# Attention on one core: zero-padded tails for scores and masks, a threshold on GpSimd, and the last tiles' logits moved into the loop

## The chip, the cores and the metric

One core of a Trainium2 chip runs the whole program. The metric is the time of one execution on the device in microseconds (us); lower is better. PE is the matrix engine, PEld its loading of stationary blocks, DVE the vector engine, ACT the scalar engine, POOL is GpSimd and SP issues most transfers. Each engine works through its own instructions in the order in which the program puts them.

## What is computed

Three stages follow one another: attention that keeps the 32 largest scores of a row, a mixture of experts whose tokens are handed out greedily by their logits, and a dense layer with a rational function. Only the first stage and the logits of the second are touched by the change.

```python
B, H, S, D = 4, 8, 576, 64            # attention
scores = q @ k.T / sqrt(D)
kth = np.partition(scores, -32, axis=-1)[..., -32:-31]
mask = scores >= kth
scores = np.where(mask, scores, -1e9)
attn = softmax(scores)                # exp(scores - max) / (sum + 1e-9)
x = (attn @ v).transpose(0, 2, 1, 3).reshape(B * S, H * D)   # 2304 x 512
logits = x @ w_gate                   # 2304 x 8, then greedy assignment
...
```

## The kernel before

**Units.** Two batches and two heads make a pass (`si`, eight of them), nine tiles of 128 queries a pass. A unit `u` is one tile with both heads; there are 72. The first head of a pair has its 64 dimensions in partitions 0 to 63, the second in 64 to 127, so both heads' scores can use the two halves of PE's rows at once. `TAIL` is 64, `MAIN` 512, `S` 576, `HS` 288.

**The loop.** `step(u)` (L1025) writes the instructions of one unit of every stage, so that the engines work on different units at a time. In the order of the program: ACT evacuates the scores of `u` (`st_evacuate`, L688); PE makes the scores of `u + 1` (`st_scores`, L673); PE turns one of five pieces of the next pass's q and k (`prepare`), which ACT copies a step later (`place`, L650); PE turns an older unit's scores and adds the mask to them (`st_transpose`, L834); DVE finds candidates (`st_candidates`, L729), and between its maxima `fill` slips in what stands in the list `later`; ACT and POOL make the window (`st_window`, L763); PE multiplies by v (`st_av`, L860); ACT and POOL make the mask (`st_weights`, L819).

**The tail of k.** The 576 keys are 512 and a tail of 64. `kT` holds 512 keys and then the tail for both heads. For the first head the scores are two matmuls of 288 columns. The second head's output wants the tail first, so it takes three, of 64, 224 and 288 (`COLS`, L228, and `TURNS`, L671): five in all.

**The mask.** Turning a unit takes nine blocks of 128 columns. The middle block (c = 4) holds the first head's tail and the second head's first 64 keys. Each block gets one transpose and one mask product with the diagonal `dg`; the middle block gets two products of half width (L844).

**The threshold.** Every third unit closes a group. From the window DVE computes the threshold `tau` and, with two operations more, the lower threshold `pn`, which ACT needs for the mask (L800 to L808). From unit 66 on each unit is a group of its own (`SG`).

**Logits.** When a tile's last pair of heads is done, the tile stands in `fresh` and then in `ready`. In units 7, 8 and 0 of a pass the loop takes one tile and computes its logits: four transposes (L912), ACT's copy and the sum of squares `xs` (L917, L919), four products (L925), DVE's copy into `lg` (L926). This happens for the first nine tiles. The last nine are done in `finish_attention` (L1094), where a small planner (`Flow`) orders the remaining work of the loop, the logits (`add_logits`, L1167) and filler work by assumed costs: three-step conversions of weights (L383 to L385) and sums of squares of weights (L306). The squares of these nine tiles come after the branch (L1473). The branch (L1303) asks whether any threshold was suspicious and reads that value on every engine; behind it the routing starts.

## Time and profile before

| | us |
|---|---|
| median of 3 runs (1241.02 to 1245.92) | 1241.24 |
| the profiled execution | 1241.38 |
| its span in the trace | 1239.6 |
| attention's loop ends (last scores done) | 416.9 |
| last instruction before the branch ends | 475.2 |
| first instruction behind the branch | 479.4 |

All times of rows count from the span's start. A row of the timeline gives start, duration, engine, line, operation, the tile that it writes and those that it reads, and how many were merged; in brackets stands how long the engine was idle before it and what it waited for. PE's durations overlap: the distance of two starts tells more than one duration. An fp32 matmul leaves two records.

### The profile page before, as it was taken

The page shows a single profiled execution, that of the slowest core. Times are in us where ns is not written, and L with a number is a line of the kernel's source. Part 1 is how long each engine was busy: PE and PEld are TensorE (multiplying, and loading weights), DVE is VectorE, ACT ScalarE, POOL GpSimd, SP SyncE. Part 2 cuts the span into 40 slices and gives each one's busy share as a digit, 9 for nine tenths or more (in the row PEclk, how much of TensorE's full clock was granted, in tenths as well). Part 3 has the DMA queues.
Part 4 walks back from the last instruction along what each step waited for, and adds up shares of the span by engine and source line. Part 5 has one row for each costly group of instructions (what it writes and reads, how often), then busy time and mean ns, then how long its engine had stood idle before and what let it go on. Part 6 is the DMA issues. An engine that isn't in the chain of part 4 may idle for free.

```text
span 1239.6 us, 27194 instructions
## 1 busy us (share of the span) xinstructions
PE 1130.0 (91%) x9879; PEld 915.3 (74%) x9879; DVE 1061.9 (86%) x4148; ACT 1019.4 (82%) x1802; POOL 375.0 (30%) x458
## 2 busy tenths in 40 slices
PE   5899999999999985884837999999999999999996
PEld 3688888888888863653625877888888888888784
DVE  6999999989898955885988979898989889897795
ACT  4899999989998985677999978888888788876684
POOL 4788777768677700001010001000101000001010
PEclk9899999999999996555868999999999999999998
DMA  5204112021100304611323222222122222100000
GB/s 124 51 10 152 41 28 50 11 50 34 27 2 2 137 2 178 234 52 55 122 88 106 99 88 88 88 82 75 32 76 88 88 74 62 41 1 21 1 20 20
DMA packets 81108, 80.63 MB, mean 65 GB/s; under 512 B 59968, under 2 KB 59968, under 8 KB 80960
## 3 DMA queue, kind: packets, MB, share of 16 engines
q1 hardware_dynamic: 77888, 69.27, 17.7%
q0 software_dynamic: 3072, 9.48, 2.6%
q8 instruction: 82, 1.34, 0.4%
q14 instruction: 66, 0.54, 0.1%
HBM read 69.25 MB, written 9.47 MB: 64 GB/s over the span
## 4 chain that ended last, share of the span: by engine, by line
PE 26%; issue 15%; ACT 7%; DVE 4%; POOL 1%; DMA 1%; POOLq 0%; DVEq 0%
PE pa L1922 3%; PE pa L1923 3%; PE pa L1924 3%; PE ph L1922 3%; PE ph L1924 3%; PE ph L1923 3%; PE po L1923 3%; PE po L1924 3%; PE po L1922 3%; ACT junk L306 2%; POOL out_dram L2308 1%; ACT w1s L1395 1%; PE pa L2297 0%; ACT wout L383 0%; DVE w2s L1400 0%
## 5 line engine op out<-in xcount | busy, mean ns | idle before, releaser
L774 POOL TENSOR_TENSOR win<-sv,sg 128x576 f32<-128x576 f32 x142 | 179.3, 1284 | 103.4 <-ACT sg L769 91.4
L738 DVE MAX8 cd<-sv 128x8 f32<-128x82 f32 (+1 forms) x1008 | 183.2, 230 | 11.2 <-ACT sv L691 8.7
L1922 PE MATMUL ph<-x,win 128*128 128x288 f16 x512 | 148.8, 291 | 10.5 <-DVE uv L2191 10.5
L873 PE MATMUL po<-vm,pT 128*128 128x65 f32 (+1 forms) x1280 | 150.5, 265 | 2.1 <-DVE x L893 1.5
L1923 PE MATMUL po<-g,wout 128*128 128x288 f16 x512 | 146.7, 287 | 2.4 <-DVE g L1913 2.4
L1924 PE MATMUL ph<-x,win 128*128 128x288 f16 x512 | 148.8, 291 | 0.0
L1923 PE MATMUL ph<-x,win 128*128 128x288 f16 x512 | 148.7, 290 | 0.0
L1922 PE MATMUL po<-g,wout 128*128 128x288 f16 x512 | 146.7, 287 | 0.9 <-ACT g L1912 0.8
L1924 PE MATMUL po<-g,wout 128*128 128x288 f16 x512 | 146.7, 286 | 0.0
L873 PEld LDWEIGHTS po<-vm,pT 128*128 128x128 f32 (+1 forms) x1280 | 138.6, 181 | 4.9 <-issue 2.1
L841 PE MATMUL pt<-ident,sv 128*128 128x128 f32 x648 | 132.0, 287 | 0.0
L845 PE MATMUL pt<-dg,mk 128*128 128x128 bf16 (+1 forms) x720 | 123.9, 225 | 0.0
L2308 POOL DMA_INDIRECT out_dram<-ob,tok x24 | 24.9, 1037 | 319.5 <-ACT ob L2304 267.5
L830 ACT ACTIVATE sg<-sv,pn 128x576 bf16<-128x576 f32 x136 | 97.8, 770 | 28.1 <-DVE pn L807 28.1
L1899 POOL DMA_INDIRECT xe<-xrows,rows_i x24 | 25.3, 1056 | 295.1 <-PE pa L1934 272.1
L769 ACT ACTIVATE sg<-sv,cut_all 128x576 bf16<-128x576 f32 x142 | 108.7, 774 | 6.2 <-DVE cut_all L744 6.1
L2182 ACT ACTIVATE z<-ph,inv 128x288 f32<-128x288 f32 x128 | 63.9, 499 | 58.7 <-PE ph L1924 57.9
L841 PEld LDWEIGHTS pt<-ident,sv 128*128 128x128 f32 x648 | 91.7, 141 | 20.8 <-issue 5.0
L775 DVE MAX8 w<-win 128x8 f32<-128x576 f32 x142 | 105.4, 743 | 0.0
L831 POOL TENSOR_SCALAR mk<-sg 128x576 bf16<-128x576 bf16 x136 | 89.5, 675 | 6.2 <-ACT sg L830 5.6
L855 ACT ACTIVATE pT<-pt 128x1152 f32<-128x1152 f32 x72 | 81.3, 1129 | 4.3 <-PE pt L845 4.0
L691 ACT ACTIVATE sv<-s 128x1152 f32<-128x1152 f32 x72 | 80.5, 1118 | 3.9 <-PE s L681 3.1
(362 smaller groups left out, 3333.2 us busy)
## 6 DMA issues: line engine op xcount, KB each, us to landing
region<-in_moe_w_dram SPq DMA_DIRECT2D x16, 2048.0 KB, 7.7
xrows<-x SPq DMA_DIRECT2D x1, 4644.0 KB
region<-in_q_dram SPq DMA_DIRECT2D x32, 128.0 KB, 2.6
region<-in_k_dram SPq DMA_DIRECT2D x32, 128.0 KB, 2.9
vm<-in_v_dram SPq DMA_DIRECT2D x32, 128.0 KB, 3.2
wout<-in_moe_w_in_dram SPq DMA_DIRECT2D x8, 511.8 KB, 8.0
region<-in_moe_w_out_dram SPq DMA_DIRECT2D x8, 511.8 KB, 3.5
win<-in_moe_w_in_dram SPq DMA_DIRECT2D x6, 511.8 KB, 7.8
```

The lines of the kernel that those rows point to most:

```text
L738: nc.vector.max(cd[:, g, :], sv[:, o : o + n])
L769: nc.scalar.activation(sg, sv_t[u, hh], AF.Sign, bias=cut_all[:, 2 * u + hh, 7:8], scale=-OVER, accum_out=t["sum"][:, c : c + 1],)
L774: nc.gpsimd.tensor_tensor(win, sv_t[u, hh], sg, op=OP.mult)
L775: later.append(lambda c=c, win=win: nc.vector.max(t["w8"][:, c, :], win))
L830: nc.scalar.activation(sg, sv, AF.Sign, bias=t["pn"][:, c : c + 1])
L831: nc.gpsimd.tensor_scalar(mk[:, hh, :], sg, -0.5, 0.5 + EPS, op0=OP.mult, op1=OP.add)
L841: nc.tensor.transpose(pt[:, c // 4, c % 4, :], pr[:, o : o + P], ident)
L845: nc.tensor.matmul(pt[p0 : p0 + n, c // 4, c % 4, :], mk[:, o + p0 : o + p0 + n], bat[b]["dg"][:, 2 * i + hh, :], start=False, stop=True, ...
L873: nc.tensor.matmul(po[p0 : p0 + n, i, hh, :], sb[:, hh * (R + 1) + c, p0 : p0 + n], vm[:, bb, hh, c, :], start=(c == 0), stop=False,)
L1922: nc.tensor.matmul(acc, ah, bh, start=first, stop=False)
L1923: nc.tensor.matmul(acc, ah, bl, start=False, stop=False)
L1924: nc.tensor.matmul(acc, al, bh, start=False, stop=last)
```

## The change

1. `kT` gets 640 columns: the tail stands behind the 512 keys for the first head and ahead of them for the second. Both heads then read two pieces of 288 columns, four matmuls for a unit. k's tail is copied in two instructions of 64 partitions. Both buffers of `kT` lie in `region`.
2. The mask of both heads lies in one of two fixed tiles with 64 columns of zeros between them. At the middle block both products are of full width: the first reads the first head's tail and the zeros, the second the zeros and the second head's first 64 keys.
3. `pn` is made by one POOL instruction from `tau`; two DVE operations a group go.
4. In the last pass every unit may take a tile's logits, and the last nine tiles count as ready once three of four pairs of heads are done. The loop then does three of four blocks of 128 columns. `finish_attention` adds the fourth block of these, and the whole of those not reached. The products there have 8 columns of output, without the turn back; the squares are done there too, those of the fourth block into `xs2`, added later.

```diff
     COLS = [
-        [(0, 0, 0, HS), (1, 0, HS, HS)],
-        [(0, 0, MAIN, TAIL), (0, TAIL, 0, HS - TAIL), (1, 0, HS - TAIL, HS)],
+        [(0, TAIL, HS), (1, TAIL + HS, HS)],
+        [(0, 0, HS), (1, HS, HS)],
     ]
...
-            kT_buf = [carve(8 * S + 2304, 2 * S), lp.tile([P, 2 * S], F32, name="kT", bufs=1)]
+            KW = S + TAIL
+            kT_buf = [carve(4 * S + 2 * KW * i, 2 * KW) for i in range(2)]
...
+            mk_buf = [wk.tile([P, 2 * S + TAIL], BF16, name=f"mk{i}", bufs=1) for i in range(2)]
+            for m in mk_buf:
+                nc.gpsimd.memset(m[:, S : S + TAIL], 0.0)
+
+            def mask_of(u, hh):
+                return mk_buf[u % 2][:, hh * (S + TAIL) : hh * (S + TAIL) + S]
...
-                    copy(kT[:, :, MAIN:S], ps[:, 1, :].rearrange("p (b c) -> p b c", b=2))
+                    tail = ps[:, 1, :].rearrange("p (b c) -> p b c", b=2)
+                    copy(kT[0:D, :, S:KW], tail[0:D])
+                    copy(kT[D:P, :, 0:TAIL], tail[D:P])
...
-            TURNS = [(1, 0), (0, 0), (1, 1), (0, 1), (1, 2)]
+            TURNS = [(1, 0), (0, 0), (1, 1), (0, 1)]
...
-                    rank, equal, lambda: pick("eqt", 1.0), lambda: pick("eqp", BEFORE),
-                    lambda: total("eqt", tau), lambda: total("eqp", t["pn"][:, g]),
+                def below():
+                    nc.gpsimd.tensor_scalar(t["pn"][:, g], tau, BEFORE, None, op0=OP.mult)
+
+                return [
+                    rank, equal, pick, total, below,
...
-                    for p0, n, hh in [(0, P, c // (R + 1))] if c != R else [(0, TAIL, 0), (TAIL, TAIL, 1)]:
+                    for hh, o in [(c // (R + 1), c * P + (TAIL if c > R else 0))] if c != R else [(0, MAIN), (1, S)]:
                         nc.tensor.matmul(
-                            pt[p0 : p0 + n, c // 4, c % 4, :], mk[:, o + p0 : o + p0 + n],
-                            bat[b]["dg"][:, 2 * i + hh, :], start=False, stop=True, skip_group_check=True,
+                            dst, mk_buf[u % 2][:, o : o + P], bat[b]["dg"][:, 2 * i + hh, :],
+                            start=False, stop=True, skip_group_check=True,
                         )
...
-                if hp == H // 2 - 1:
+                if hp == H // 2 - (1 if bp < B // 2 - 1 else 2):
                     fresh.extend(range(t0, t0 + n))
+                elif hp == H // 2 - 1:
+                    final.extend(range(t0, t0 + n))
...
+            def chunks_of(t):
+                return whole if t < NT - NJ else whole[: KC - 1]
...
-                pending = ready.pop(0) if ready and getting is None and j in (7, 8, 0) else None
+                pending = ready.pop(0) if ready and getting is None and (j in (7, 8, 0) or si == NSI - 1) else None
...
                 def add_logits(t, deps):
...
+                    cs = whole[KC - 1 :] if t in counted else whole
...
+                    def product():
+                        for i, c in enumerate(cs):
+                            nc.tensor.matmul(
+                                st["ps"][:, 1, 0:E], st["xt"][:, i, :], wg[:, c, :], start=(i == 0), stop=(c == last_c)
+                            )
+
+                    def leave():
+                        if n == 1:
+                            nc.vector.tensor_tensor(lg[:, t, :], st["ps"][:, 1, 0:E], lg[:, t, :], op=OP.add)
                         else:
...
-        norms = [
-            flow.add("A", 0.52, lambda t=t: square(x[:, t, 0:DM], xs[:, t : t + 1]), (), XSR) for t in late_tiles
-        ]
...
-            everywhere_steps(xs, OP.max, x_max) + [("V", 0.07, f) for f in power_steps(s_x, i_x, x_max, 388)],
-            norms, -85.0,
+            [("V", 0.1, lambda: nc.vector.tensor_tensor(xs, xs, xs2, op=OP.add))]
+            + everywhere_steps(xs, OP.max, x_max) + [("V", 0.07, f) for f in power_steps(s_x, i_x, x_max, 388)],
+            [], -85.0,
```

POOL, in the middle of the loop, around the end of a group (`win` is the window, `top_all` and `dg` the diagonal, `mk` the mask). Before:

```order
L774 TENSOR_TENSOR win<-sv,sg 128x576 x2
L757 TENSOR_SCALAR top_all<-top 128x6
L758 TENSOR_TENSOR dg<-identb,top_all 128x768
L831 TENSOR_SCALAR mk<-sg_691 128x576
L831 TENSOR_SCALAR mk<-sg_694 128x576
L774 TENSOR_TENSOR win<-sv,sg 128x576 x2
```

With the change:

```order
L787 TENSOR_TENSOR win<-sv,sg 128x576 x2
L770 TENSOR_SCALAR top_all<-top 128x6
L771 TENSOR_TENSOR dg<-identb,top_all 128x768
L844 TENSOR_SCALAR mk_172<-sg_683 128x576
L844 TENSOR_SCALAR mk_172<-sg_686 128x576
L821 TENSOR_SCALAR pn<-tau_all 128x6
L787 TENSOR_TENSOR win<-sv,sg 128x576 x2
```

`pn` stands behind the old group's masks and ahead of the next unit's two windows.

ACT, behind the loop, from the spill of `pT` for unit 67 to that for unit 68 and on to the next (L383 to L385 and L306 are filler). Before:

```order
L855 ACTIVATE pT<-pt 128x1152
L383 ACTIVATE win<-win 128x512 x2
L384 ACTIVATE win<-win 128x512 x2
L385 ACTIVATE win<-win,bias_111 128x512 x2
L383 ACTIVATE win<-win 128x512
L855 ACTIVATE pT<-pt 128x1152
L384 ACTIVATE win<-win 128x512
L306 ACTIVATE win,wsum<-region 128x1024
L385 ACTIVATE win<-win,bias_111 128x512
L383 ACTIVATE win<-win 128x512
L306 ACTIVATE win,wsum<-region 128x1024
L855 ACTIVATE pT<-pt 128x1152
```

With the change (the squares of a fourth block are L1221):

```order
L867 ACTIVATE pT<-pt 128x1152
L1221 ACTIVATE sg,xs_132<-x 128x128 x2
L383 ACTIVATE win<-win 128x512
L1221 ACTIVATE sg,xs_132<-x 128x128 x2
L384 ACTIVATE win<-win 128x512
L383 ACTIVATE win<-win 128x512
L1221 ACTIVATE sg,xs_132<-x 128x128
L385 ACTIVATE win<-win,bias_111 128x512
L867 ACTIVATE pT<-pt 128x1152
```

The filler is the same in number, spread otherwise over the spills, and nine squares come in between: seven over 128 columns and, near the end, two over 512. The loop itself takes seven of the last nine tiles.

## Rows read from the trace of the kernel before

**Rows 1.** The page: clock in tenths, 40 slices of the span

```profile
PEclk9899999999999996555868999999999999999998
```

**Rows 2.** Windows: stretch, length, busy us (instructions) of each engine, PEclk, DMA share, GB/s

```profile
172.09:222.97 50.88, 50.88 (x491) 44.01 (x489) 48.37 (x298) 46.84 (x79) 39.37 (x42) 1.00 0.16 37
...
277.83:332.69 54.86, 54.86 (x527) 48.08 (x526) 48.40 (x300) 49.93 (x88) 39.26 (x42) 1.00 0.15 34
...
387.54:416.88 29.34, 28.81 (x267) 24.47 (x267) 29.09 (x182) 27.16 (x46) 23.93 (x29) 1.00 0.01 1
```

**Rows 3.** Waits of DVE and of ACT from 70 to 223 us: total, times, longest

```profile
DVE den L891 <- PE po L877: 3.1, 8, 0.6
...
ACT sg L830 <- DVE pn L807: 9.0, 9, 1.1
```

**Rows 4.** Timeline of PE in one unit: scores, transposes with masks, products with v

```profile
415.60 1.35 PE L681 MATMUL s<-kT,region 64*128 64x64 f32 x10
416.88 0.33 PE L841 MATMUL pt<-ident,sv 128*128 128x128 f32 x1
...
417.44 0.28 PE L841 MATMUL pt<-ident,sv 128*128 128x128 f32 x1
417.56 0.22 PE L845 MATMUL pt<-dg,mk 128*128 128x128 bf16 x1
417.61 0.28 PE L841 MATMUL pt<-ident,sv 128*128 128x128 f32 x1
417.82 0.25 PE L845 MATMUL pt<-dg,mk 128*64 128x128 bf16 x2
418.00 0.33 PE L841 MATMUL pt<-ident,sv 128*128 128x128 f32 x1
...
418.22 0.28 PE L841 MATMUL pt<-ident,sv 128*128 128x128 f32 x1
...
420.97 0.28 PE L841 MATMUL pt<-ident,sv 128*128 128x128 f32 x1
```

**Rows 5.** Timeline of POOL, DVE, ACT and PE at a group's end

```profile
129.81 0.24 POOL L757 TENSOR_SCALAR top_all<-top 128x6 f32<-128x6 f32 x1
...
132.87 2.53 POOL L774 TENSOR_TENSOR win<-sv,sg 128x576 f32<-128x576 f32 x2
...
134.15 0.18 DVE L807 TENSOR_REDUCE tau_all<-eqt 128x6 f32<-128x48 f32 x1
134.41 0.18 DVE L807 TENSOR_REDUCE pn<-eqp 128x6 f32<-128x48 f32 x1
134.62 1.44 ACT L830 ACTIVATE sg<-sv,pn 128x576 bf16<-128x576 f32 x2 [1.08 <-DVE pn L807]
...
135.97 1.11 ACT L691 ACTIVATE sv<-s 128x1152 f32<-128x1152 f32 x1
...
138.08 0.74 DVE L775 MAX8 w<-win 128x8 f32<-128x576 f32 x1
138.93 1.35 PE L681 MATMUL s<-region 64*128 64x64 f32 x10
```

**Rows 6.** Groups of ACT and DVE by line and form, 223 to 388 us

```profile
L919 ACT ACTIVATE sg<-x 128x512 bf16<-128x512 f32 x9 | 5.7, 635 | 0.0
L917 ACT ACTIVATE xt<-s 128x512 f32<-128x512 f32 x9 | 5.3, 594 | 0.0
...
...
L926 DVE COPY lg<-po 128x8 f32<-128x8 f32 x9 | 1.5, 167 | 16.0 <-PE po L925 16.0
```

**Rows 7.** Windows behind the loop, columns as in rows 2

```profile
428.34:459.45 31.11, 29.05 (x277) 24.39 (x277) 19.49 (x61) 30.47 (x39) 1.00 (x1) 1.00 0.04 15
442.32:454.47 12.15, 11.63 (x105) 9.74 (x105) 6.23 (x20) 12.15 (x17) 0.00 (x0) 1.00 0.01 2
```

**Rows 8.** Timeline behind the loop: a spill of ACT, the last logits on DVE

```profile
442.32 1.13 ACT L855 ACTIVATE pT<-pt 128x1152 f32<-128x1152 f32 x1 [0.54 <-PE pt L845]
...
475.02 0.17 DVE L1212 COPY lg<-s 128x8 f32<-128x8 f32 x1 [0.36 <-PE s L1200]
```

More of the change, by code (lines that the diff above doesn't have):

```diff
@@ L497 @@
         xs = xpool.tile([P, NT], F32, name="xs")
+        xs2 = xpool.tile([P, NT], F32, name="xs2")
+        nc.gpsimd.memset(xs2, 0.0)
         tau_all = xpool.tile([P, NTILE], F32, name="tau_all")
@@ L659, in place @@
                 if step in (2, 3):
[L660 removed]
+                    copy(kT[:, bb, TAIL:S].rearrange("p (r c) -> p r c", c=P), ps, True)
                     return
@@ L821, in st_weights @@
                 t = bat[b]
-                mk = wk.tile([P, 2, S], BF16, name="mk", bufs=2)
                 for hh in range(2):
@@ L1061, in step @@
                     placing.append((si + 1, getting))
-                if pending is not None:
-                    logits_transpose(pending, beside(sc_t[u + 1]))
+                if pending is not None and u + 1 < NU:
+                    logits_transpose(pending, beside(sc_t[u + 1]), chunks_of(pending))
                     turning.append(pending)
@@ L1175, in turn @@
                         st["xt"] = wk.tile([P, KC, P], F32, name="xt", bufs=2)
-                        for c in range(KC):
+                        for i, c in enumerate(cs):
                             nc.tensor.transpose(
-                                st["ps"][:, 0, c * P : (c + 1) * P], x[:, t, c * P : (c + 1) * P], ident
+                                st["ps"][:, 0, i * P : (i + 1) * P], x[:, t, c * P : (c + 1) * P], ident
                             )
-                    def copy(h):
-                        o = slice(h * 2 * P, (h + 1) * 2 * P)
-                        src, dst = st["ps"][:, 0, o], st["xt"].rearrange("p c x -> p (c x)")[:, o]
-                        if h and XA:
-                            nc.scalar.activation(dst, src, AF.Copy)
-                        else:
-                            nc.vector.tensor_copy(dst, src)
@@ L1189, in product, with copy @@
-                    def product(h):
-                        for c in (2 * h, 2 * h + 1):
+                    def copy():
+                        nc.vector.tensor_copy(
+                            st["xt"].rearrange("p c x -> p (c x)")[:, 0 : n * P], st["ps"][:, 0, 0 : n * P]
+                        )
+                    def product():
+                        for i, c in enumerate(cs):
                             nc.tensor.matmul(
-                                st["ps"][0:E, 1, 0:P], wg[:, c, :], st["xt"][:, c, :], start=(c == 0), stop=(c == KC - 1)
+                                st["ps"][:, 1, 0:E], st["xt"][:, i, :], wg[:, c, :], start=(i == 0), stop=(c == last_c)
@@ L1193, in product @@
                             )
                     def leave():
-                        st["lt"] = wk.tile([E, P], F32, name="lt", bufs=2)
-                        nc.vector.tensor_copy(st["lt"], st["ps"][0:E, 1, 0:P])
-                    def back():
-                        nc.tensor.transpose(st["ps"][:, 1, P : P + E], st["lt"], ident[0:E, 0:E])
-                    p = last.add("P", 0.5, turn, deps, LR + t)
-                    ps = [p]
-                    vs = []
-                    for h in range(2):
-                        vs.append(last.add("A" if h and XA else "V", 0.35, lambda h=h: copy(h), [p], LR + t))
@@ L1207, in add_logits @@
-                    ps = last.add("P", 0.43, lambda: product(0), vs[0:1], LR + t)
-                    ps = last.add("P", 0.43, lambda: product(1), [ps, vs[1]], LR + t)
-                    v = last.add("V", 0.2, leave, [ps], LR + t)
-                    b = last.add("P", 0.1, back, [v], LR + t)
-                    hold(v, "lt", 2, [b])
-                    v = last.add("V", 0.1, lambda: nc.vector.tensor_copy(lg[:, t, :], st["ps"][:, 1, P : P + E]), [b], LR + t)
+                        if n == 1:
+                            nc.vector.tensor_tensor(lg[:, t, :], st["ps"][:, 1, 0:E], lg[:, t, :], op=OP.add)
+                        else:
+                            nc.vector.tensor_copy(lg[:, t, :], st["ps"][:, 1, 0:E])
@@ new lines, in norm_of @@
+                    def norm_of():
+                        junk = wk.tile([P, S], BF16, name="sg")
+                        nc.scalar.activation(
+                            junk[:, 0 : n * P], x[:, t, cs[0] * P : DM], AF.Square,
+                            accum_out=(xs2 if n == 1 else xs)[:, t : t + 1],
+                        )
+                    a = last.add("A", 0.3 if n == 1 else 0.7, norm_of, deps, 900 + t)
+                    hold(a, "sg", 3, [a])
+                    p = last.add("P", 0.15 * n, turn, deps, LR + t)
@@ L1213, in add_logits @@
+                    v = last.add("V", 0.1 + 0.14 * n, copy, [p], LR + t)
+                    ps = last.add("P", 0.25 * n, product, [v], LR + t)
+                    v = last.add("V", 0.15, leave, [ps], LR + t)
                     take(p, s_users[t % 2], 1, [v])
                     hold(p, "xt", 2, [ps])
-                    late_tiles.append(t)
                     return v
```

74 lines of the change are left out of this document (36 added, 38 removed).

## Prediction

> **What bounds the kernel now.** I read the page first, for the clock by slice [rows 1]: up to 465 us, the attention part (15 slices of 31 us), PE runs at the upper of its two levels (2.4 GHz; the 5s further on are 1.2 GHz), so times of one stretch there hold for the others. The stretches come next [rows 2]: each of the first two is one pass of nine units, cut at the start of a score group. A pass without logits takes 50.9 us and PE has no gap in it; DVE is idle 2.5 us of it, ACT 4.0, POOL 11.5. A pass with three tiles' logits takes 54.9 us, again all PE, and DVE and ACT have 6.5 and 4.9 us to spare. The view of waits decides [rows 3]: between 70 and 223 us PE has no wait of its own at all, while DVE waits for PE (8 times for `den`, 3.1 us) and ACT waits for DVE's `pn` once a group of three units, 9.0 us in nine times. So the chain runs PE, DVE, ACT; PE sets the pace; and the next engine is DVE, not 5% behind. After the loop another bound holds: from the spill of `pT` at 442.32 to the second one after it, at 454.47, ACT is busy 12.15 of 12.15 us, so a spill comes every 6.1; its filler ends at 459.4, and then the last logits go to and fro between PE and DVE until 475.2 [rows 7, 8].
>
> **The change part by part.** Durations are those of the profiled execution, which took 1241.4 us (span 1239.6); the median of the three runs shown is 1241.2, so both stand for each other.
>
> *Scores.* Five matmuls take 415.60 to 416.88, 1.28 us [rows 4]; four will do the same columns, 576 for each of the two halves of 64 rows. By columns nothing is saved, by number a fifth, 0.26 us. I take the middle, 0.13 us a unit.
>
> *Mask at the middle block.* A transpose and its mask product come every 0.17 us (417.44 to 417.61). Around the two half-width products it is 0.39 (417.61 to 418.00) and 0.22 in the pair after: 0.27 us too much. The new form has one more full-width product there, and a product costs the next transpose 0.05 us (417.56 to 417.61). So about 0.21 us a unit goes; if the second product cost a whole pair's 0.17, it would be 0.10. One rule speaks against this. The Trainium skill, "TensorEngine Tiling (Array Packing)", section "When to Use Tiling", has two stationary blocks of up to 64 columns work side by side, a gain of up to two. By that rule the pair of half-width products already costs no more than one, and padding both with zeros to full width would lose 0.05 us a unit instead of saving 0.21. The row decides for me: the half-width pair is the dearest thing in the group.
>
> *What the loop gives.* 0.34 us a unit (0.10 to 0.48) is 3.1 us a pass for PE alone, 22 us over the 66 units from 43 to 388 us. DVE allows less. Without logits it can give up what it waits for PE, 3.1 us in three passes [rows 3] or 1.0 a pass, and the two operations that the change takes from each of three groups (0.18 long like the one at 134.41 [rows 5], of which about half overlaps the next: 0.6): 1.6, and a little of the idle time that no wait explains. I take 2.0 for each of three passes, and 2.8 for each of the three with logits, where DVE and ACT have more room; 1.2 for the five units after 43 us. Together 15.6 us (4 to 22.4).
>
> *The threshold by POOL.* `tau` stays where it is on DVE or moves up a little (134.15, 0.18 long); then comes a POOL instruction over 128x6, like the one at 129.81, 0.24 us [rows 5]. With the handovers `pn` is there near 134.5, where DVE's own ended at 134.59. So ACT's threshold pass, at 134.62, starts no later. But `pn` stands ahead of the next pair of windows on POOL, which started at 132.87 and will now start near 134.5 and end near 137.0. The later of the two maxima that read it comes at 138.08, with 1.1 us left; the masks behind it move by the same 1.6, and PE reads them only with the transposes behind the scores of 138.93. Covered, but if POOL were 1.1 us later, DVE would stand still.
>
> *Smaller edits.* k's tail is copied by two instructions over 64 partitions instead of one, one more a pass on ACT, at most the 0.59 us of a copy of 512 columns [rows 6]; ACT has 4.0 idle. The zeros between the masks are written once, at the start, when POOL has time. SP's queue keeps its order.
>
> *Logits in the last pass.* Seven tiles get three of four blocks there. In the passes with logits a tile costs (54.86 - 50.88) / 3 = 1.33 us [rows 2], so 1.0 for three blocks. Five units and one score group of the last pass keep PE busy for 28.81 us, (28.81 - 1.28) / 5 = 5.5 a unit, so they come to 5.5 - 0.34 + 1.0 = 6.2 at most. ACT has at most 27.16 / 5 = 5.4 a unit of its own there and gets three quarters of 0.59 and 0.64 [rows 6], 6.3 in all, and has the wait for `pn` each unit. DVE's copy of the logits waits for PE (16.0 us in nine times [rows 6]), and the next unit's candidates are queued behind it. I take 0.75 a unit on top of the old pace, 5.3 us (3.5 to 8).
>
> *The tail.* From 459.4 to 475.2 only logits run [rows 8]: each tile is four transposes, two copies, four wide products, a copy, a turn back, a copy. Seven now need one block, two need four, in a chain without the turn back. PE's chain alone would end near 459.7: four units of 3.9 for transposes and products (416.88 to 420.97 less the 0.21 [rows 4]) and 1.5 for the spill (1.13 at 442.32 [rows 8]) with its two handovers, 5.4 instead of 6.1, then 4.5 for the last tile. ACT is later. From 428.34 to 459.45 it is busy 30.47 of 31.11 us [rows 7], and it gets nine squares: seven over 128 columns (a quarter of the columns of a square of 0.64 [rows 6], so between 0.16 and 0.64; I take 0.4, since a start and a read are in each) and two over 512 with their reads, 0.75 each: 4.3 us. So ACT ends at 463.7 and the branch, now behind 475.19, comes 11.5 us earlier (6, if fillers hold each spill back a unit's share; 15.5 with PE's chain).
>
> *Behind the branch.* The branch costs what it did. ACT's nine squares behind it, 0.75 each, are gone; the routing that follows goes between DVE and PE, so I count 0.5 (0 to 3). PE's clock is at the lower level in the slices from 496 us on, when the branch has left PE idle [rows 1]; it will fall there too, so nothing is counted.
>
> Sum: 1241.4 - 15.6 + 5.3 - 11.5 - 0.5 = 1219.1.
>
> **The rivals.** No change that a measurement can tell apart means within 0.5%, 6.2 us.
> - *DVE stops the loop.* Its 5% of idle time may be handovers that no faster PE gives back. Then the loop gains little more than its two operations, 4 us, and the time is 1241.4 - 4 + 5.3 - 11.5 - 0.5 = 1230.7. For it: DVE's waits for PE are short and many; against: they carry PE's name. 14%.
> - *PE alone counts.* The loop gives 22.4, the tail PE's chain of 15.5, the routing 2: 1206.8. Against it stands ACT's full tail. 15%.
> - *Half-width products run side by side.* The mask edit costs 0.05 instead of saving 0.21, and 0.08 a unit is left, 5 us: 1229.7. Against: the 0.27 us of [rows 4]. 5%. (It is what the Trainium skill, "TensorEngine Tiling (Array Packing)", section "When to Use Tiling", would make of the edit.)
> - *The logits don't leave the way, they move.* Seven units in a row with DVE's copy behind PE may cost 1.7 us each instead of 0.75, 12 us in all: 1225.8. The 16.0 us of waits speak for it, PE's closed ranks in those passes against. 5%.
> - *Slower, by POOL.* The threshold ahead of the window pair delays masks and maxima. PE's slack at a group's end is 1.85 us (the evacuation of 135.97 ends at 137.08, the scores start at 138.93 [rows 5]), so it decides once `pn` comes that much later. To end 6.2 us above 1241.4 the loop must lose 12.9 us against before instead of gaining 15.6, over 23 groups 0.56 each, so `pn` 2.4 us late: about 1248. The row of 0.24 speaks against it. 3%.
>
> **How the numbers follow.** The forecast, 1212 to 1226 with 1219.1 likeliest, has 55%; 3% are for what I don't see. The range 1208 to 1231 takes in the forecast, the logits rival, the page's rule, most of DVE's rival and a part of PE's. Faster by over 0.5% is all but the slower rival and the edges above 1235: 0.93; same 0.04; slower 0.03.
>
> **What would show it.** After: score groups of 1.15 us and no pair of 0.39 at the middle block; a pass without logits of about 48.9 us and one with logits of 52.1; PE with short waits, DVE over 97% busy; the last pass 5 us longer; ACT's last filler some 4 us before the branch's end moves, and no chain of logits behind it. The prediction is wrong if score groups stay at 1.28 us, if DVE's maxima wait for POOL's windows, or if the tail still ends over 50 us behind the last scores.

## The result, and the profile after

| | before | after |
|---|---|---|
| median, us | 1241.45 (1241.02 to 1245.92, 4 runs) | 1226.91 (1222.19 to 1231.60, 4 runs) |
| ratio to before | | 0.9875, 95% interval 0.9831 to 0.9919 |
| the profiled execution, and its span | 1241.38, 1239.6 | 1231.60, 1229.9 |

The change is worth 14.5 us where 22.3 was forecast; 1226.9 lies in the range of 1208 to 1231 and 0.9 above the likeliest 1212 to 1226. The execution profiled first is the slowest of the four. A second one, told of below, took 1225.86 us (span 1224.1) and stands beside it here. Cut at four points of the program, the spans differ from before's by (us):

| | forecast | first profile | second |
|---|---|---|---|
| loop, to the second unit of the last pass (387.54 before) | -15.6 | -17.2 | -15.4 |
| from there to the start of the last scores (415.6) | +5.3 | +3.5 | +3.4 |
| from there to the first instruction behind the branch (479.4) | -11.5 | **+3.6** | **-3.8** |
| from there to the end (760.2 long) | -0.5 | +0.4 | +0.3 |
| sum | -22.3 | -9.7 | -15.5 |

The loop came as forecast or better; the tail, the stretch from the last scores to the branch, did not. (Of the seven tiles whose logits moved, PE makes five in the second stretch and two behind the start of the last scores, at 408.7 and 414.3 us in the first profile. So of the +5.3 some 3.8 belong to the second row and 1.5 to the third.) The page of the changed kernel, the clock in 40 slices, answers to [rows 1]:

```profile
PEclk9899999999999765555969999999999999999998
```

The clock falls two slices sooner, some 60 us. The windows (columns as in [rows 2]) are a pass without logits, one with, the units up to the last scores, and, for [rows 7], ACT's stretch from the first spill of `pT` behind the loop (ACT's copy of a unit's turned scores) to its last filler:

```profile
166.08:214.15 48.07, 48.02 (x469) 41.78 (x469) 47.12 (x292) 46.76 (x80) 39.89 (x45) 1.00 0.17 39
266.09:318.03 51.94, 51.94 (x506) 45.85 (x505) 47.47 (x294) 50.06 (x89) 39.88 (x46) 1.00 0.16 36
370.30:401.89 31.59, 30.84 (x290) 27.45 (x289) 27.31 (x173) 30.65 (x59) 23.99 (x33) 0.99 0.01 1
419.62:464.71 45.09, 40.52 (x265) 36.00 (x264) 20.35 (x68) 34.86 (x57) 1.83 (x2) 0.65 0.00 1
```

PE is still without a gap in both passes (50.88 to 48.07, 54.86 to 51.94), so PE, not DVE, still sets the loop. In the tail PE has a mean clock of 0.65, where before it had 1.00, and ACT, which filled 30.47 of 31.11 us, is idle for 10 of 45. The longest of ACT's waits there is not for PE:

```profile
428.50 0.31 ACT L1221 ACTIVATE sg<-x 128x128 bf16<-128x128 f32 x1 [5.76 <-DVE x L905]
```

One of the nine new squares stands at the head of ACT's queue until DVE has made `x`, with filler queued behind it. DVE in turn had waited 4.86 us for PE's products with v, at the lower clock. Such waits of squares come to 7.1 us in the stretch, those of spills for PE's transposes to 3.2; in the second profile they are 2.0 and 1.4.

PE's timeline in one unit, for [rows 4] (a row with x2 merges the two full-width products of the middle block):

```profile
388.56 1.24 PE L694 MATMUL s<-region 64*128 64x288 f32 x8
389.74 0.55 PE L931 MATMUL s<-ident,x 128*128 128x128 f32 x3
...
390.65 0.28 PE L853 MATMUL pt<-ident,sv 128*128 128x128 f32 x1
390.77 0.22 PE L857 MATMUL pt<-dg,mk 128*128 128x128 bf16 x1
390.83 0.28 PE L853 MATMUL pt<-ident,sv 128*128 128x128 f32 x1
390.94 0.28 PE L857 MATMUL pt<-dg,mk 128*128 128x128 bf16 x2
391.05 0.28 PE L853 MATMUL pt<-ident,sv 128*128 128x128 f32 x1
```

Scores take 1.18 us from start to start, and the step over the middle block is 0.22 (390.83 to 391.05) where it was 0.39, with nothing lost in the pair behind it.

The waits from 64 to 214 us, for [rows 3] (total, times, longest):

```profile
POOL pn L821 <- DVE tau_all L818: 5.6, 10, 0.9
ACT sg L843 <- POOL pn L821: 4.5, 4, 1.2
...
DVE cd L751 <- ACT sv L704: 2.9, 12, 0.4
```

DVE no longer waits for PE's `den`; the new chain runs from DVE's threshold over POOL to ACT, and in the middle of the loop it is covered: PE waits once in these 150 us, 0.7 us for ACT.

The place where the tail begins is not. DVE, POOL and PE there:

```profile
409.50 0.17 DVE L946 COPY lg<-po 128x8 f32<-128x8 f32 x1 [2.18 <-PE po L945]
...
412.23 0.22 POOL L821 TENSOR_SCALAR pn<-tau_all 128x2 f32<-128x2 f32 x1 [2.52 <-DVE tau_all L818]
412.42 2.52 POOL L787 TENSOR_TENSOR win<-sv,sg 128x576 f32<-128x576 f32 x2
...
415.90 1.31 POOL L844 TENSOR_SCALAR mk<-sg 128x576 bf16<-128x576 bf16 x2
...
416.62 0.29 PE L857 MATMUL pt<-dg,mk 128*128 128x128 bf16 x1 [1.41 <-POOL mk L844]
```

DVE's copy of a tile's logits waits 2.18 us for PE's product, with the maxima of the next unit queued behind it; the threshold is late by that, POOL's `pn` waits 2.52 us for it with the windows queued behind it, the masks are late, and PE stands (below, such idle time of PE is called a stop). Part of the 2.18 us is the clock's doing, since PE's product stands behind scores that were made at the lower level; in the second profile, where the clock holds there, the last two such copies wait 1.09 and 0.78 us, `pn` 2.06 and 1.12. The clock around it, as windows of the same profile:

```profile
402.00:404.00 2.00, 2.00 (x8) 1.07 (x8) 2.00 (x8) 2.00 (x6) 0.50 (x1) 0.50 0.00 0
...
408.00:415.00 7.00, 6.12 (x60) 5.79 (x59) 5.31 (x35) 4.27 (x9) 4.41 (x6) 1.00 1.02 394
...
416.00:428.00 12.00, 11.38 (x83) 10.37 (x84) 6.94 (x15) 3.53 (x10) 5.15 (x7) 0.50 0.06 22
...
432.00:448.00 16.00, 15.04 (x76) 13.39 (x77) 8.04 (x23) 13.49 (x21) 0.00 (x0) 0.51 0.00 1
```

It falls to the lower level (0.50) near 402, is up again, and is low from 415.1 for most of the time up to 449. Before, it held the upper one until 472.5, through this stop:

```profile
428.82 1.08 PE L873 MATMUL po<-vm,pT 128*128 128x65 f32 x8 [1.55 <-DVE x L893]
```

### The profile page after: what moved, and what is told of

Its sections match the earlier page's. It is cut to its first block, busy times and chain, and to the rows that moved or that the text cites. A ratio compares the mean times of both kernels' runs of the same rounds, so it can differ in the third digit from the quotient of the medians.

```text
span 1229.9 us, 26889 instructions
## 1 busy us (share of the span) xinstructions
PE 1119.1 (91%) x9710; PEld 912.3 (74%) x9710; DVE 1050.9 (85%) x4084; ACT 1022.8 (83%) x1831; POOL 379.9 (31%) x488
## 4 chain that ended last, share of the span: by engine, by line
PE 27%; issue 15%; ACT 7%; DVE 4%; POOL 1%; DMA 0%; POOLq 0%; DVEq 0%
PE pa L1936 3%; PE pa L1937 3%; PE pa L1938 3%; PE ph L1936 3%; PE ph L1937 3%; PE ph L1938 3%; PE po L1937 3%; PE po L1938 3%; PE po L1936 3%; ACT junk L306 2%; POOL out_dram L2322 1%; ACT w1s L1412 1%; PE pa L2311 0%; ACT wout L383 0%; DVE w2s L1417 0%
## 5 line engine op out<-in xcount | busy, mean ns | idle before, releaser
L751 DVE MAX8 cd<-sv 128x8 f32<-128x82 f32 (+1 forms) x1008 | 177.7, 228 | 12.0 <-ACT sv L704 11.9
L885 PE MATMUL po<-vm,pT 128*128 128x65 f32 (+1 forms) x1280 | 157.3, 273 | 1.7 <-DVE eqt L815 0.9
L885 PEld LDWEIGHTS po<-vm,pT 128*128 128x128 f32 (+1 forms) x1280 | 144.9, 188 | 5.0 <-DVE eqt L815 1.1
L857 PE MATMUL pt<-dg,mk 128*128 128x128 bf16 x720 | 125.0, 226 | 1.4 <-POOL mk L844 1.4
L2196 ACT ACTIVATE z<-ph,inv 128x288 f32<-128x288 f32 x128 | 63.8, 499 | 59.0 <-PE ph L1938 58.2
L694 PE MATMUL s<-region 64*128 64x288 f32 (+1 forms) x640 | 93.7, 442 | 15.8 <-ACT region L665 12.3
L853 PEld LDWEIGHTS pt<-ident,sv 128*128 128x128 f32 x648 | 95.7, 148 | 15.0 <-ACT sg L782 3.1
```

Of the source, the lines that this page charges most:

```text
L694: nc.tensor.matmul(sc[p0 : p0 + n, 2 * hh + g, 0:w], qT[rows, j, p0 : p0 + n], kT[rows, bb, c : c + w], start=True, stop=True,)
L751: nc.vector.max(cd[:, g, :], sv[:, o : o + n])
L853: nc.tensor.transpose(dst, pr[:, c * P : (c + 1) * P], ident)
L857: nc.tensor.matmul(dst, mk_buf[u % 2][:, o : o + P], bat[b]["dg"][:, 2 * i + hh, :], start=False, stop=True, skip_group_check=True,)
L885: nc.tensor.matmul(po[p0 : p0 + n, i, hh, :], sb[:, hh * (R + 1) + c, p0 : p0 + n], vm[:, bb, hh, c, :], start=(c == 0), stop=False,)
```

## The experiments

Twelve runs followed, one of the changed kernel as it is and two of one edited kernel (both2). In this table "spill" is the time from the start of the last scores to the first spill of `pT` behind the loop, "tail" that to the first instruction behind the branch, both from the run's profile; the ratio is to the runs of the kernel before on the same chip, whose medians there were 1243.2 to 1245.8.

| run | median | ratio | last scores at | spill | tail |
|---|---|---|---|---|---|
| (before) | 1241.45 | 1 | 415.6 | 11.7 | 63.8 |
| (after, first profile) | 1226.91 | 0.9875 | 401.9 | 17.7 | 67.4 |
| again | 1226.25 | 0.9855 (0.9817 to 0.9894) | 403.5 | 15.0 | 60.1 |
| loop12 | 1229.84 | 0.9892 (0.9859 to 0.9926) | 400.9 | 11.6 | 64.1 |
| late | 1226.28 | 0.9873 (0.9834 to 0.9912) | 397.1 | 13.7 | 65.6 |
| pn_dve | 1238.25 | 0.9952 (0.9934 to 0.9969) | 414.5 | 13.4 | 63.4 |
| lg_later | 1220.01 | 0.9809 (0.9781 to 0.9838) | 401.0 | 13.2 | 55.4 |
| pn_last2 | 1224.74 | 0.9851 (0.9820 to 0.9881) | 403.0 | 15.3 | 59.2 |
| both2 | 1217.61 | 0.9792 (0.9764 to 0.9820) | 399.7 | 12.5 | 56.7 |
| both2b | 1216.57 | 0.9773 (0.9745 to 0.9802) | 402.3 | 12.5 | 56.5 |
| nosq | 1223.24 | 0.9832 (0.9803 to 0.9860) | 404.2 | 16.2 | 57.4 |
| sus_late | 1219.91 | 0.9799 (0.9772 to 0.9826) | 400.2 | 12.5 | 58.5 |
| late2 | 1227.32 | 0.9888 (0.9850 to 0.9926) | 396.4 | 11.6 | 70.5 |
| warm | 1228.81 | 0.9889 (0.9866 to 0.9911) | 403.2 | 19.0 | 61.4 |

**again**: the changed kernel, no edit.

> The changed kernel once more, nothing edited. Theory A: what was lost behind the loop is TensorE's clock, which fell at 401.7 us and again at 415.4 us, each time some microseconds behind a short stop of PE (398.0 to 398.8; 411.1 to 412.0 and 415.1 to 416.6), while the kernel before kept the upper level through stops of up to 1.8 us until 472.5; so the loop up to 370 us repeats within 0.2 us, and the time swings by several microseconds with the places at which the clock falls: 1222 to 1232 us. Theory B: the same fixed instructions bring it down each time: the clock falls at 401.7 and 415.4 again and the branch comes at 464.4 within 0.5 us.

Windows of its profile (396 to 428, then on), and ACT's stretch from the first spill:

```profile
396.00:428.00 32.00, 26.36 (x266) 23.53 (x266) 28.74 (x144) 26.05 (x53) 20.45 (x30) 1.00 0.36 133
428.00:433.00 5.00, 4.72 (x22) 4.51 (x23) 2.13 (x6) 5.00 (x6) 0.00 (x0) 0.58 0.00 0
...
418.53:457.14 38.61, 33.33 (x262) 29.75 (x262) 21.12 (x65) 34.83 (x57) 3.14 (x3) 0.81 0.00 1
```

The same instructions with stops of the same length (0.91 and 1.41 us, both for POOL's masks; 0.88 for DVE and 1.41 for a mask before), but the clock stays up to 428 us. Behind the first spill ACT's stretch is 38.6 us instead of 45.1: 6.5 us between two executions of one program, which differ in the clock and in ACT's idle time (10.2 and 3.8 us). The longest stop of the kernel before was 1.55 us and not 1.8. So the falls at 401.5 and 415.1 us are not fixed by the program, and 1222 to 1228 us was the spread again. The loop did not repeat within 0.2 us: it is 1.8 longer, from one dip of the clock (last section). The runs of the kernel before swing the same way: of 13 on this chip the two at a mean clock of 0.933 and 0.934 took 1240.1, the three at 0.919 took 1247.0 to 1247.2.

**loop12**: the kernel before with parts 1 and 2 alone.

```diff
-        [(0, 0, MAIN, TAIL), (0, TAIL, 0, HS - TAIL), (1, 0, HS - TAIL, HS)],
+        [(0, 0, HS), (1, HS, HS)],
...
-  for p0, n, hh in [(0, P, c // (R + 1))] if c != R else [(0, TAIL, 0), (TAIL, TAIL, 1)]:
+  for hh, o in [(c // (R + 1), c * P + (TAIL if c > R else 0))] if c != R else [(0, MAIN), (1, S)]:
...
```

> The kernel before with parts 1 and 2 alone (four score matmuls, zeros between the masks); pn stays DVE's two operations and all last logits stay behind the loop. Theory A (PE set the pace and DVE was never near): the units take 5.58 and 5.14 us as in the whole change, the last pass starts near 370.3 us, the last scores end near 398, the tail keeps its length of 58 us, so the time is 1241.4 - 19 = 1222, as fast as the whole change or faster. Rival, as my sum had it (DVE caps the loop): a pass without logits takes 48.9 to 49.4 us instead of 48.1, and the time is 1228 to 1231.

A pass of it without logits:

```profile
147.20:195.89 48.69, 48.02 (x470) 41.80 (x470) 47.85 (x298) 46.85 (x80) 39.16 (x43) 1.00 0.17 39
```

Neither fits whole. PE's units are as short as in the whole change (5.58 and 5.14), but a pass takes 48.69, between the two forecasts, and DVE is busy for 47.85 of it. The 0.6 us more are one wait of PE, and the chain behind it starts at DVE's `pn`:

```profile
165.72 1.44 ACT L841 ACTIVATE sg<-sv,pn 128x576 bf16<-128x576 f32 x2 [1.33 <-DVE pn L818]
167.07 1.11 ACT L702 ACTIVATE sv<-s 128x1152 f32<-128x1152 f32 x1
168.23 1.24 PE L692 MATMUL s<-region 64*128 64x288 f32 x8 [0.67 <-ACT sv L702]
```

ACT's threshold pass waits for `pn`, the evacuation of the scores behind it is late, and so are PE's next scores. With its two operations for `pn` DVE does begin to bind, by 0.6 us in each pass without logits; PE has no such wait in the passes with logits. Parts 1 and 2 give most of the change's gain, 1229.8; the tail kept its length (64.1).

**late**: all last logits behind the loop.

```diff
-                if hp == H // 2 - (1 if bp < B // 2 - 1 else 2):
+                if hp == H // 2 - 1 and bp < B // 2 - 1:
```

> The changed kernel, but all nine last tiles' logits behind the loop, in the tail's new form, and their squares with them. Theory A (DVE's copy of the logits waits for PE with the window's maxima queued behind it, so threshold, masks and at last PE stand still, and then the clock falls): PE's stops in the last pass shrink to at most 0.8 us, the clock keeps its upper level at least to 425 us, the last scores end near 398 us, and the time is 1217 to 1224. Rival (pn on POOL makes the stops): the mask product behind the loop still waits over 1 us for POOL and the clock falls near there; 1226 to 1232.

The rival has it. The stop is there without any of the last tiles' logits in that pass:

```profile
403.65 0.23 PE L857 MATMUL pt<-dg,mk 128*128 128x128 bf16 x1 [1.27 <-POOL mk L844]
```

and the clock's mean is 0.57 from 404 to 408 us. So POOL's queue alone can make the stop, and theory A, which had only DVE's copy, is not the whole. (In late2, below, `pn` is DVE's again in these units and no logits stand in the pass either: PE waits for no mask, and the spill comes at 11.6 as in the kernel before.) The median says more: 1226.3 with all logits behind the loop, 1226.9 and 1226.3 with seven tiles' in it. As the change stood, moving them gained nothing that these runs can tell; the forecast gave it 6.2 us, 11.5 less 5.3.

**pn_dve**: `pn` by one DVE instruction.

```diff
-                    nc.gpsimd.tensor_scalar(t["pn"][:, g], tau, BEFORE, None, op0=OP.mult)
+                    nc.vector.tensor_scalar(t["pn"][:, g], tau, BEFORE, None, op0=OP.mult)
```

> The changed kernel with pn made by one DVE instruction in place of POOL's. Theory A (the queue behind DVE's copy is what delays the masks): the last pass and the tail stay as they are, the mask product still waits 1 to 1.5 us near 415 us, 1222 to 1232 us, no difference beyond the spread. Rival (POOL's pn, which holds the windows behind it back by 1 to 2.5 us, is the cause): the windows start 1 to 2 us earlier in the last pass, the wait of the mask product is under 0.5 us, the clock stays up past 425 us and the time is 1216 to 1221.

A miss for both: 12 us slower. The loss is in the loop, a pass without logits and DVE's group for `pn` in 166 to 213 us (busy, mean ns):

```profile
147.85:197.57 49.72, 48.19 (x470) 41.77 (x469) 49.28 (x295) 46.87 (x80) 39.12 (x43) 1.00 0.17 38
```

```profile
L821 DVE TENSOR_SCALAR pn<-tau_all 128x6 f32<-128x6 f32 x3 | 2.3, 779 | 0.0
```

Six elements a partition take 0.78 us, where a reduction over 48 took 0.18 [rows 5]: the instruction stands while POOL's window runs (last section). With it DVE is full, 49.28 of 49.72, and sets the pace. The edit tried a dearer form than the kernel before had, so it doesn't price the move to POOL; loop12 does.

**lg_later**: DVE's copy of the logits goes into the list `later`.

```diff
-                nc.vector.tensor_copy(lg[:, t, :], acc)
+                later.append(lambda: nc.vector.tensor_copy(lg[:, t, :], acc))
...
```

(The lines left out empty the list in the code that runs only for a suspicious threshold.)

> The changed kernel; DVE's copy of a tile's logits goes into the list from which the next unit's maxima are interleaved, instead of standing ahead of them. Theory A (the maxima stand behind a copy that waits for PE): DVE has no wait over 0.5 us for the logits product in the last pass (1.1 and 2.2 us before the last two units now), POOL's pn waits under 0.7 us for the threshold instead of 1.1 to 2.5, PE waits under 0.5 us for POOL's masks instead of 0.9 and 1.4, the first spill behind the loop starts within 14 us of the last scores' start (15.0 and 17.7 in the two profiles of the changed kernel), and the time falls by 2 to 4 us. Rival (pn ahead of the windows in POOL's queue): PE's waits for the masks stay over 0.7 us and the time stays within 1.5 us.

The only stop that PE has left from 398 to 415 us:

```profile
412.49 0.23 PE L857 MATMUL pt<-dg,mk 128*128 128x128 bf16 x1 [0.68 <-POOL mk L844]
```

DVE's copy no longer waits for the product, the spill comes at 13.2, the tail is 55.4 us and the time falls by 6 us, more than expected; the slowest of its four runs (1221.5) is below the fastest of the changed kernel's eight (1222.2). POOL still waits 1.1 us for the threshold and PE 0.68 for a mask, as they were not to. Theory A holds for the larger part.

**pn_last2**: in the six single-unit groups `pn` by DVE's two operations, as before.

```diff
...
+                if n == 2:
+                    return [rank, equal, pick, pick_below, total, total_below]
                 return [
                     rank, equal, pick, total, below,
```

> The changed kernel; for the six groups of one unit at the end pn is made by DVE's two operations of the kernel before, for all others by POOL. Rival theory (POOL's queue): POOL's windows in the last pass start when the sign passes of ACT are done and not behind the threshold, 1 to 2 us earlier; PE's waits for POOL's masks fall under 0.5 us and the time by 2 to 4 us. Theory A (DVE's copy ahead of the maxima): threshold and masks come as late as before, PE's waits stay over 0.7 us, the time stays within 1.5 us. In both the loop up to 370 us is that of the changed kernel, 48.1 us a pass without logits.

POOL's windows and DVE's copy in it:

```profile
403.34 2.52 POOL L787 TENSOR_TENSOR win<-sv,sg 128x576 f32<-128x576 f32 x2 [1.09 <-ACT sg L782]
```

```profile
410.79 0.17 DVE L957 COPY lg<-po 128x8 f32<-128x8 f32 x1 [2.23 <-PE po L956]
```

The windows now start behind ACT's sign pass and PE waits for no mask, as the rival said, but DVE's copy stands as long as in the first profile (here too the clock was low just ahead of it, from 403.2 us), and PE waits for DVE instead (1.11 us, then 1.70 for `x`, ahead of products with v). The time is 1.5 and 2.2 us below the changed kernel's two medians, and its runs (1222.8 to 1226.8) lie among that kernel's: undone alone, POOL's queue is worth nothing that these runs can tell.

**both2, both2b**: both edits, twice.

> The two edits of the last two runs together. If both queues matter: PE has no wait over 0.5 us for a mask up to the first spill behind the loop, that spill starts 11 to 13 us behind the last scores' start (11.7 in the kernel before), and the median is 1219 to 1223 us, 3 to 6 below the changed kernel. If only one matters, this run is as fast as that one, within 1 us.

> The kernel with both edits once more, as the neighbour of the next one. Theory A: 1216 to 1219 us again, the first spill behind the loop 12 to 13 us behind the last scores' start. If its lead over the changed kernel was only a lucky clock, it comes out at 1222 or more.

The spill comes at 12.5 in both, PE has one stop of 0.67 us ahead of it, and 1217.6 and 1216.6 are 9 us below the changed kernel's two medians. The intervals (0.9764 to 0.9820, 0.9745 to 0.9802) lie below the changed kernel's (0.9831 to 0.9919, 0.9817 to 0.9894), but for an overlap of 0.0003, and all nine runs (1212.8 to 1219.1) are below its eight: this version beats both kernels. The two queues add up: 6 us for DVE's, and some 2 to 3 more for POOL's once the first is out of the way. The second figure is less sure, since the intervals of lg_later and both2 overlap.

**nosq**: no squares behind the loop (the sums of squares of the last nine tiles lack a block or all four).

```diff
...
-                    a = last.add("A", 0.3 if n == 1 else 0.7, norm_of, deps, 900 + t)
-                    hold(a, "sg", 3, [a])
```

> The changed kernel without the nine squares behind the loop (the sums of squares of the last nine tiles lack one block or all four). My sum had ACT's filler set the end of the tail, with 4.3 us for the squares: the branch comes 4 to 4.5 us earlier, and the median is near 1222. Rival (the end hangs on PE's and DVE's chain at the lower clock and ACT stands still in between, over 8 us in the first profile): under 1.5 us.

Between the two: 3.0 us less than `again`, the branch 2.1 earlier. Two spills of ACT in it:

```profile
420.40 1.13 ACT L868 ACTIVATE pT<-pt 128x1152 f32<-128x1152 f32 x1 [3.12 <-PE pt L858]
436.93 1.13 ACT L868 ACTIVATE pT<-pt 128x1152 f32<-128x1152 f32 x1 [2.42 <-PE pt L858]
```

Where ACT has less to do it waits for PE, and it no longer waits for DVE's `x`. The squares account for 2 to 3 of the 4.3 us; the four runs of either kernel spread over 3 to 5 us, so this run says no more.

**sus_late**: both edits, and the check for suspicious thresholds later.

```diff
...
-                checked = last.add("V", 0.6, lambda: suspicious(), [w for d in win_of.values() for w in d], 250)
+                checked = last.add("V", 0.6, lambda: suspicious(), [w for d in win_of.values() for w in d] + wgt_of[NU - 1][-1:], 250)
```

> Both edits, and the check for suspicious thresholds (five DVE operations, 420.4 to 421.9 us in the profile of both2) waits for the last unit's masks. Theory C (PE's 1.9 us stop at 420.5, where it waits for DVE's sum of logits behind that check, is on the path, and the clock falls behind it): the stop is under 0.8 us, the clock keeps its upper level to 430 us, the fourth spill behind the last scores' start comes 2 to 4 us earlier, and the median falls by 1.5 to 4 us to 1214 to 1216. Rival (ACT's filler is the bound there, or the clock falls without that stop): within 1 us of its neighbour.

A miss, 3 us above its neighbour both2b, with runs that overlap (1216.7 to 1221.3 against 1212.8 to 1219.1), so no faster at least:

```profile
421.41 0.33 PE L1211 MATMUL s<-ident,x 128*128 128x128 f32 x1 [0.38 <-DVE lg L1228]
423.41 1.44 PE L896 MATMUL po<-vm,pT 128*128 128x65 f32 x8 [1.67 <-ACT pT L878]
```

PE's stop of 1.9 us is gone, and PE stops 1.67 us for ACT's spill instead, which stands behind filler; the clock falls at 424, where it fell at 422.5 and 425.1 in the two profiles of both2. ACT is the bound at that point, as the prediction said of the tail, but not with work alone:

```profile
418.74 0.31 ACT L1234 ACTIVATE sg<-x 128x128 bf16<-128x128 f32 x1 [2.90 <-DVE x L916]
```

A square had held ACT's queue for 2.90 us, ahead of that filler and of the spill (2.89 in both2). No run moves the squares; what that would give is open.

**late2**: both edits, and all last logits behind the loop, the edits of lg_later, pn_last2 and late together.

> The kernel with both edits, but all of the last nine tiles' logits behind the loop: what part 4 of the change is worth once the two queues no longer stop PE. As my sum had it (11.5 us gained in the tail, 5.3 given in the last pass): 5 to 7 us slower than with the logits in the loop (1216.2 and 1216.6 for the two medians of that kernel... taken as 1217), so 1222 to 1224. Rival (the logits only moved): 1216 to 1219.

The medians that it quotes as 1216.2 and 1216.6 are 1217.6 and 1216.6. It took 1227.3, some 10 us more. Its end, with PE at the lower level all through:

```profile
450.00:462.00 12.00, 9.69 (x42) 8.19 (x42) 3.15 (x12) 4.04 (x8) 0.00 (x0) 0.50 0.00 0
```

So with the queues mended the logits in the loop are worth 10 us where 6 were forecast, and with the queues as they were nothing (late): what is left behind the loop also runs at half the clock.

**warm**: PE filled with idle products where it stood.

```diff
...
+                keep_busy({67: 16}.get(u, 0))
...
+                keep_busy({63: 9, 65: 9}.get(u, 0))
...
```

> The changed kernel with idle products of PE (64 columns, nothing reads them) where it stood still in the last pass: 9 ahead of the products with v of units 63 and 65, 16 ahead of the first transposes behind the loop, some 0.1 us each. Theory (PE's stops bring its clock down some microseconds later): the clock keeps its upper level from 396 to 424 us, the mean clock of the runs rises (0.914 to 0.923 in the eight runs of the changed kernel), and the median falls to 1222 to 1225. Rival (the clock falls there or not, whatever PE does in these stops): clocks as before, and the median stays at 1226 or rises by up to 1.5 us, since not all of the products are covered.

One of the fillers, and the clock:

```profile
411.90 2.17 PE L859 MATMUL s<-ident 128*128 128x64 f32 x18
```

```profile
392.00:432.00 40.00, 36.41 (x360) 33.93 (x358) 30.90 (x165) 29.18 (x57) 22.97 (x33) 1.00 0.29 106
```

The clock stayed up to 432 us, as the theory had it; but `again` kept it to 428 without any filler, so one profile doesn't show the cause. An idle product cost 0.22 us (two records), not 0.1, the spill came 4 us later behind the last scores' start than in `again`, and the median rose to 1228.8. Whether filling the stops holds the clock stays open.

The profiles together say a little more about where it falls. In nine of them (both of the changed kernel, pn_dve, lg_later, pn_last2, both2, both2b, nosq, warm) PE has the same longer stop in the tail, where it waits for DVE's sum of a tile's logits:

```profile
422.43 0.46 PE L1211 MATMUL s<-ident,x 128*128 128x128 f32 x1 [1.90 <-DVE lg L1228]
```

It ends at 422.43 us here, in both2, and the clock falls at 422.5. In eight of the nine the fall comes within 1.9 us behind the stop's end, in the first profile within the stop. That is an order in time and not yet a cause: the kernel before kept its clock through 1.55 us, and in sus_late, which lacks this stop, the clock fell 0.6 us behind another of 1.67.

## Why the prediction was right, and where it failed

The total came into the range because the loop came (17.2 and 15.4 us in the two profiles, 15.6 forecast). What part 4 was to bring on top, 6.2 us net, did not show in the change as it stood (`late`).

**Scores: right.** 0.13 us forecast, 0.11 measured (1.28 to 1.17).

**Mask at the middle block: right, and the rule wrong here.** 0.21 forecast; the transposes of a unit went from 1.86 to 1.65 us without preparation and from 1.80 to 1.59 with it, by 0.21. The rule in the Trainium skill, "TensorEngine Tiling (Array Packing)", section "When to Use Tiling", by which the half-width pair already ran side by side, would have made the unit longer. The measurement decides against it in this place.

**What the loop gives: right mechanism, the cap too low.** With PE's 0.33 us a unit nearly all of PE's gain came through, 2.8 us a pass without logits and 2.9 with (2.0 and 2.8 forecast). The step "DVE allows less" was sound without part 3: in loop12 DVE holds the pass without logits at 48.69. It failed because the two operations taken from DVE count in full; POOL's `pn` buys 0.6 us there. The 22 us for PE alone had a slip: between 43 and 388 us stand 59 units and not 66, as the prediction's own sum over passes has it, so PE alone was worth 20 at 0.34 a unit.

**The threshold by POOL: covered in the loop, not at its end.** The working was made at one place, a group of three units at 134 us, where 1.1 us were left. In the last pass each unit is a group, and `late` shows the stop of 1.27 us there without any logits of these tiles.

**Logits in the last pass: right in size (3.5 where five of seven tiles make 3.8), incomplete in where the bill comes.** "The next unit's candidates are queued behind it" was the right sentence, and its cost was put inside the pass. It came out behind it: the spill behind the loop is 17.7 and 15.0 us after the last scores' start instead of 11.7, 3.3 to 6.0 us of which the sum had 1.5, for the other two tiles. lg_later takes the copy out of the way, the spill comes at 13.2, 1.5 behind the old, and the time falls by 6 us.

**The tail: this step failed.** "So ACT ends at 463.7" counted ACT's 32.1 us of work and waiting behind the first spill plus 4.3, 36.4; the profiles show 45.1 and 38.6, since ACT waits for PE and for DVE's `x`. By the prediction's own sign (a tail that "still ends over 50 us behind the last scores") this part was wrong: the last instruction ahead of the branch ends 60.5 and 53.8 us behind them, 58.3 before. The squares were sized right as durations (0.41 and 0.75 us each with a read), but they also wait, up to 5.76 us, with filler queued behind them. And the clock is missing: "so times of one stretch there hold for the others" was read from the kernel before and carried over, and "so nothing is counted" looked only behind the branch. The stretch is 8.7 and 2.2 us longer than the sum, at a mean clock of 0.65 and 0.81. How much of that is the clock and how much the queues no run takes apart, and the clock goes with the spread of the runs only in part: of the changed kernel's eight the slowest has the lowest mean, 0.914, and the two fastest 0.921 and 0.922, but one at 0.923 took 1225.9. Against `both2` (tail 56.7, forecast 52.3) some 4 us of the forecast gain are still missing; the clock's mean there is 0.54 from 422 to 428. (The rival end of 459.7 for PE's chain names no start, so its sum cannot be redone.)

**Behind the branch: nothing**, inside the 0 to 3 (760.2 us before, 760.6 and 760.5 after; 758 to 762 in all fourteen profiles).

The rivals: DVE's stop of the loop did not come with part 3 in place; PE alone was right for the loop in its mechanism (17.2 and 15.4 where it had 22.4) and wrong for the tail; "the logits move", at 1225.8, was nearest to the median, and in its mechanism too, though the place was the handover to the tail (it had 5%); POOL's lateness, priced for the loop's groups, decided only in the last six.

## What to carry to other kernels

When work is moved into a loop, look at the first wait behind it on each engine's queue and ask what stands there at the loop's end, where groups get smaller and cover goes. Price a moved instruction by its wait as well as by its length. A copy that waits for another engine's late result belongs behind the work that others wait for: one copy moved gave 6 us, and with the second queue 9, more than half of what the whole change gave. Where a gain rests on a stretch in which the clock held, price that stretch at the lower level too, for the range.

## What was not expected

**The clock dips with PE busy all the time.** In `again` the loop's one slow unit, in a pass with logits:

```profile
311.46 1.01 PE L945 MATMUL po<-wg,xt 128*128 128x8 f32 x8
312.39 2.03 PE L694 MATMUL s<-region 64*128 64x288 f32 x8
```

```profile
312.70:316.10 3.40, 3.40 (x19) 2.13 (x16) 3.40 (x19) 2.01 (x6) 1.18 (x3) 0.50 0.02 5
```

PE has no gap there, and the scores behind the eight records of 8-column products take 1.96 us instead of 1.17, at the lower level, which holds from 312.7 to 316.1 us. Four of the fourteen profiles have such a dip between 44 and 375 us, five dips in all, always right behind the products of a unit with logits (near 260, 313 or 359 us); the fall at 401.5 us in the first profile stands behind such products too. That these thin products bring the clock down was not tested. The Trainium skill, "TensorE: Matmul & The Clock Gate", section "Part 1: The HAM clock gate", lets the clock follow how busy PE has been; a busy PE as the profile counts it did not keep it here.

**DVE's `tensor_scalar` and POOL shut each other out.** The masks of two units on DVE and POOL's pair of windows in the first profile, and the same masks in both2, where only the first meets POOL:

```profile
418.08 4.12 DVE L828 TENSOR_SCALAR mk<-sv,tau_all 128x576 bf16<-128x576 f32 x4
...
418.51 2.94 POOL L1141 TENSOR_TENSOR win<-sv,sg 128x576 f32<-128x576 f32 x2
```

```profile
412.62 2.36 DVE L839 TENSOR_SCALAR mk<-sv,tau_all 128x576 bf16<-128x576 f32 x4
```

Alone a mask takes 0.51 us; two of the four beside POOL's windows took 1.53 each, and POOL's pair 2.94 instead of 2.52. That is what made `pn` cost 0.78 us in pn_dve. A pair of windows and `pn` beside it there, and the one `pn` that met no POOL instruction:

```profile
149.69 2.52 POOL L787 TENSOR_TENSOR win<-sv,sg 128x576 f32<-128x576 f32 x2
149.99 1.01 DVE L821 TENSOR_SCALAR pn<-tau_all 128x6 f32<-128x6 f32 x1
...
417.32 0.15 DVE L821 TENSOR_SCALAR pn<-tau_all 128x2 f32<-128x2 f32 x1
```

The first window ends at 150.97, `pn` at 151.00; in every group of pn_dve up to 377 us it ends 0.02 to 0.04 us behind a window's end. The Trainium skill, "SBUF — State Buffer", section "Who interferes with whom", says it: a DVE operation of that kind can take the pair of ports that it shares with GpSimd, and the later of the two waits for the whole instruction. The trace agrees.
